# Attention and two MoE layers on one core: other planner constants, masks loaded first through another buffer, last output tile in halves

## The chip, the cores and the metric

The kernel runs on one core of a Trainium2 chip. The metric is the device time of one execution in microseconds (us). Three executions of the kernel before took 864.69, 868.79 and 866.26 us; their median is 866.26 us. One more was profiled and took 865.21 us, of which 863.4 us lie between its first and its last instruction (the span).

## The reference, cut to what matters

Inputs are q, k, v of shape (4 batches, 8 heads, 576 positions, 64), in float32, and weights in float64.

```
out_d     = softmax(mean4(q) @ mean4(k).T / 8) @ mean4(v)     # 144 pooled positions, repeated 4 times
out_local = softmax(where(|i - j| < 4, q @ k.T / 8, -1e9)) @ v  # a narrow band
x = (repeat4(out_d) + out_local), laid out as 2304 tokens x 512
h = x @ w_in (512 x 2048);   x = (h * cos(h)) @ w_out (2048 x 512)
out = ((x @ w1) * (x @ w2)) @ w3 @ w_out2    # 512 x 1024 twice, 1024 x 1024, 1024 x 512
```

## The kernel before, in words

**The work.** Weights arrive as 64-bit words and are turned into float32 on the chip: ScalarE and VectorE (`w_job`) take the two halves of each word apart and put a float32 together, three instructions for a block of 128 x 512. The products of the MoE layers run as three matmuls of split values (`mm3`). The last two weight matrices are first multiplied with each other (`w5_job`, tile `ps_w`, 128 matmuls of 128x512 in two halves r = 0 and 1), and the eight results go to a DRAM scratch `w5_sc` (shown as `w_sc`), issued by ScalarE. Attention is done by units of 192 positions (`unit_job`: the band) and by pairs of heads (`pair_job`: the pooled part, with `pool_v_job` for its values). Two units make a chunk of 384 tokens; a chunk's x feeds `h_job` (`ps_h`), a chain on ScalarE, VectorE and GpSimd (`chain_job`: turns, sine, square, g) and `y_job` (`ps_y`). After all six chunks the second layer runs (`ab_job`: `ps_ab`, `o_job`: `ps_o`), by three chunks of 768 tokens with six output tiles each.

**The planner.** Nothing is scheduled on the chip: while the program is built, a planner (`run`) keeps a clock for each engine, estimates every instruction (`cost`) and the delay until others see it (`LATENCY`), and gives each free engine the job with the lowest urgency whose inputs the plan holds ready. What comes out is a fixed order for each engine, and on the chip an engine that waits holds up all that stands behind it. The urgency of a job is a base plus one of the `U_` constants: of attention's loads of q and k, its pairs, its pooled values and its units, and of w_in, w_out and the second half of w3. The base of the first chunk's attention is `A0`; blocks j of the first half of w3 and of w4 have j - 0.5 and j - 1. Matmuls of `w5_job` have urgency 900, those of `h_job` 1016 and of `y_job` 1016.5, so on TensorE the product of the weights goes ahead of h where both are ready. `HALF` is the number of w_in blocks that chunk 0 goes through before chunk 1 starts. `SLACK` is how long a buffer must have been free in the plan before a load into it is issued. `exps` collects exponentials while ScalarE's table holds the sine, until `TOGETHER` of them wait or the first has waited `PATIENCE` ns. While TensorE has nothing to do early on, the planner puts matmuls of zeros there (`warm_up`, `ps_z`).

**The start.** ScalarE's queue issues six small DMAs: two for an identity matrix, four for the masks (`bands_raw`). SyncE issues q, k, v and weights, all on its own queue. `bands_raw` lies in buffer 0 of the ring `raw`; the same memory is taken next for `qkd`, the pooled q and k, which VectorE writes first of all. Then ScalarE casts the masks (`bands`) and scales the identity (`ident_r`); the first two units (`BANDS`) add the masks on TensorE and need both. 

**The end.** `o_out_job` copies a finished output tile from PSUM, on ScalarE for even tiles and VectorE for odd ones, and SyncE stores it.

Nearly every instruction is issued through the recorder at L131, so the profile's groups are told apart by tiles and not by lines; DMAs of ScalarE stand under L125.

Of the kernel before, what the change touches and what calls it, by code (L numbers as in the profile page):

```python
# [13 lines left out]
I64 = mybir.dt.int64  # L14
AF = mybir.ActivationFunctionType
# [6 lines left out]
P = 128  # L22
DM = H * D
# [12 lines left out]
QS = 64  # L36
KS = QS + 2 * HALO
# [5 lines left out]
N2 = 768  # L43
NH = N2 // 2
NCH2 = NT // N2
NQ = 7
HALF = 10
SCALE = 1.0 / math.sqrt(D)
TWO_PI = 2.0 * math.pi
LAG = 3  # L50
WARM = 256
EARLY_WARM, RISEN, REST = 3000.0, 10000.0, 130.0
FIRST, SLACK = 3000.0, 1000.0
TOGETHER, PATIENCE = 3, 6000.0
A0, A1 = 11, 4

U_QK, U_PAIR, U_POOL, U_UNIT = -13, -12, -11.5, -8
U_WI, U_WO, U_W3 = -4, -0.5, -1
OUT_BANKS = (4, 5, 6, 7, 2, 3)
EARLY = 2  # L60
BIAS, BANDS = 2, 4
LATENCY = {"pe": 200, "se": 140, "ve": 130, "ge": 150, "sy": 2000}


def band_of(u, w):
# [5 lines left out]
def fused_kernel(ctx: ExitStack, tc: tile.TileContext, qk_block, v_block, qk_pool, v_pool,  # L71
# [8 lines left out]
    def size(a):  # L80
        return math.prod(a.shape[1:])

    def cost(name, op, out, ins, func):
        n = max(size(a) for a in [out] + ins)
        if name == "ve":
            shared = n > 64 and ends["ge"] > max(now[0], ends["ve"])
            if op.startswith("tensor_scalar") and len(ins) == 1:
                return 90 + n * (1.5 if shared else 0.65)
            both = len(ins) == 2 and n > 64 and not any(a.tensor.name.startswith("ps_") for a in ins)
            return 75 + n * (2.2 if both and shared else 1.17 if both else 1.04)  # L90
        if name == "se":
            load = 1283 if func in (AF.Exp, AF.Sin) and func != table[0] else 0
            table[0] = func if load else table[0]
            return (60 if ins[0].tensor.name.startswith("ps_") else 100) + n / 1.2 + load
        if name == "ge":
            return 160 + (1.7 if any(0 in [step for step, _ in a.ap] for a in ins) else 2.3) * n
        if name == "sy":
            return max(450, n * out.shape[0] * (8 if out.dtype == I64 else 4) / 310)
        n = size(out)
        if op == "transpose":  # L100
            return 70
        if ins[0].dtype == F32R:
            return 12.5 + n / 2.4
        return (4 if ins[0].shape[0] == P else 2) * max(35, n / 2.4)

    def visible(a):

        end, by = written.get(a.tensor.name, (0.0, "pe"))
        return end + LATENCY[by]

# [24 lines left out]
    ve, se, pe, ge, sy = (Engine(*e) for e in (("ve", nc.vector), ("se", nc.scalar), ("pe", nc.tensor), ("ge", nc.gpsimd), ("sy", nc.sync)))  # L135
# [18 lines left out]
    ident_r = const.tile([P, P], F32R, name="ident_r")  # L154
    bands = const.tile([P, 3, KS], F32R, name="bands")
# [11 lines left out]
    def buf(slot, name, shape, dtype=F32):  # L167

        pool, size, _ = slots[slot[0]]
        item = 8 if dtype == I64 else 4  # L170
        t = pool.tile([P, size // item], dtype, name=name, tag=f"{slot[0]}{slot[1]}", bufs=1)
        t = t[:, :math.prod(shape)]
        if len(shape) == 1:
            return t
        names = "abcd"[:len(shape)]
        return t.rearrange(f"p ({' '.join(names)}) -> p {' '.join(names)}", **dict(zip(names, shape)))
# [27 lines left out]
    def on(name, fn, *aps, when=lambda: True):  # L204
        yield name, fn, aps, when

    def until(cond):
        while not cond():
            yield "until", cond
# [26 lines left out]
    def give(name, slot, engine):  # L236
        free[name].append((ends[engine] + LATENCY[engine], slot))

# [4 lines left out]
    def count(key, n=1):  # L243
        done[key] = done.get(key, 0) + n

    def reached(key, n):
        return lambda: done.get(key, 0) >= n
# [535 lines left out]
    def plan():  # L783

        f = 0
        while f < F1:
            if f >= HALF:
                yield from until(lambda: reached(("x", 1), UPC)() or ("wi", f) in w_t)
# [250 lines left out]

    def o_out_job(j, t, ps):  # L1040
        slot, name = (yield from take("t")), "ve" if t % 2 else "se"
        o = buf(slot, "o", [DM])
        yield from on(name, lambda: ve.tensor_copy(o, ps) if t % 2 else se.copy(o, ps), ps)
        give(f"bank{OUT_BANKS[t]}", 0, name)
        yield from on("sy", lambda: sy.dma_start(out=out[j * N2 + t * P:j * N2 + (t + 1) * P, :], in_=o), o)
        give("t", slot, "sy")
        count("out")

    with tc.manual_schedule():
        z = buf(("turns", 0), "zeros", [WARM])  # L1050
        ge.memset(z, 0.0)
        zr = z.bitcast(F32R)
        warmed = [(bank(7, "ps_z"), True)]

        def warm_up():

            if warmed[0] is None:
                if done.get("w5", 0) < F2 or not at_hand("bank7"):
                    return False
                ps, alone = bank(7, "ps_z"), True  # L1060
            else:
                ps, alone = warmed[0]
            pe.matmul(ps[:, :WARM], lhsT=zr[:, :P], rhs=zr, start=alone, stop=alone)
            ends["pe"] += REST if now[0] > RISEN else 0
            return True

        idle.append(warm_up)

        W5 = 2 * F2
        first, seen = {}, []  # L1070
        first.update({i: HALF if i == 1 else F1 * i for i in range(NC1)})
        first.update({("f", f): f if f < HALF else f + HALF for f in range(F1)})

        def attention(i, at):

            for b in sorted({(UPC * i + m) // UPB for m in range(UPC)} - set(seen)):
                seen.append(b)
                if b < EARLY:
                    for m in range(UPB):
                        Job(at + U_QK + 0.5 * m, unit_qk_job(UPB * b + m))  # L1080
                for p in range(KC):
                    Job(at + U_PAIR + 2 * p, pair_job(b, p))
                    Job(at + U_POOL + 2 * p, pool_v_job(b, p))
            for m in range(UPC):
                Job(at + U_UNIT + 3 * m, unit_job(UPC * i + m))

        ge.memset(ident, 0.0)
        se.dma_start(out=ident[:QB, :QB], in_=ident_in)
        se.dma_start(out=ident[QB:, QB:], in_=ident_in[:P - QB, :P - QB])
        raw = buf(("raw", 0), "bands_raw", [3, KS])  # L1090
        for half in (slice(0, QS), slice(QS, P)):
            se.dma_start(out=raw[half, :2], in_=bands_in[:QS, :2, :KS])
            se.dma_start(out=raw[half, 2], in_=bands_in[QB - QS:, 2, QB - QS:])
        se.copy(bands, raw)
        se.activation(out=ident_r, in_=ident, func=AF.Copy, scale=1.0 / SCALE)
        ends["sy"] = FIRST
        attention(0, A0)
        for j in range(F2):
            Job(j - 1, w_job(("w4", j), w4[j]))
            Job(j - 0.5, w_job(("w3", 0, j), w3t[0, j]))  # L1100
        for j in range(F2):
            Job(F2 + j + U_W3, w_job(("w3", 1, j), w3t[1, j]))
        Job(900, w5_job())
        for f in range(F1):
            Job(W5 + first["f", f] + U_WI, w_job(("wi", f), w_in[f]))
            Job(W5 + first["f", f] + U_WO, w_job(("wo", f), w_out[f]))
        Job(W5 + 1000, h_job(W5))
        Job(W5 + 1000.5, y_job())
        attention(1, W5 + first[1] - A1)
        for i in range(2, NC1):  # L1110
            run(reached("h", first[i - 1] + 1 if i > 2 else first[0] + HALF + 1))
            attention(i, W5 + first[i])
            if i == 2:
                for f in range(F2):
                    Job(W5 + first[2] + 4 * f, w12_job(f))
        run(lambda: done.get("h", 0) > first[NC1 - 1] and done.get("w12 begun", 0) == F2)
        at_stack.close()
        p2 = ctx.enter_context(tc.tile_pool(name="p2", bufs=1))
        slots.update({"x2": (p2, 4 * KC * N1, 6), "v": (p2, 4 * NH, 2)})
        free["x"] += [(0.0, ("x2", n)) for n in range(6)]  # L1120
        free["v"] = [(0.0, ("v", n)) for n in range(2)]
        base = W5 + NSTEPS
        for n in range(F2 * NQ // 2):
            Job(base + 2 * n / NQ - 8, back_job(n))
        for n in range(len(steps2)):
            Job(base + n - 6, w5_back_job(n))
        Job(base - 8, y_in_job(0))
        Job(base + 1000, ab_job(base))
        Job(base + 1000.5, o_job(base))
        run(reached("out", NT // P))  # L1130
# [53 lines left out]
```

## Time and profile before

| | us |
|---|---|
| median of 3 runs (lowest to highest) | 866.26 (864.69 to 868.79) |
| the profiled execution | 865.21 |
| its span | 863.4 |
| TensorE (PE) busy | 842.7 |
| VectorE (DVE) busy | 503.3 |
| ScalarE (ACT) busy | 446.9 |
| GpSimd (POOL) busy | 366.6 |

PE counts as busy while a matmul is in flight, and matmuls overlap; so the busy share says where PE had nothing at all, and the pace of a known group (a row "x12" with its length) says where it was slow. "Idle before" is followed by what ended it. In a timeline a row merges equal instructions that follow each other.

### The profile page before, as it was taken

Reading aid. Unit: us, or ns where it says so; the run is one execution under the profiler, and the core shown is the slowest. Engines: PE = TensorE matmul, PEld = TensorE weight load, DVE = VectorE, ACT = ScalarE, POOL = GpSimd, SP = SyncE. Lnnn points to the kernel's source line nnn. Section 1 sums busy time; section 2 is a strip of 40 time slices with the busy share of each in tenths; the row PEclk is TensorE's granted clock in tenths of the full one; section 3 lists DMA queues with packets and bytes.
Section 4 is the critical chain, followed back from the end, with each engine's and each line's share of the span. In section 5 each row is a group of like instructions: output and inputs, shape, how many; then the busy total and the mean of one; then the engine's idle time right before and its main releaser. Section 6 shows DMA issues by size and latency. Waiting matters only on the chain.

```text
span 863.4 us, 14938 instructions
## 1 busy us (share of the span) xinstructions
PE 842.7 (98%) x5627; PEld 760.4 (88%) x5627; DVE 503.3 (58%) x897; ACT 446.9 (52%) x908; POOL 366.6 (42%) x330
## 2 busy tenths in 40 slices
PE   8999989999999999999999999999999999999998
PEld 6454579989999899999999999999999899989997
DVE  5988687985537883787356434715335633364332
ACT  2655689876766775677667556651113311231111
POOL 0013677746442445245425344524334633363333
PEclk8999989999999999999999999999999999999999
DMA  9989982131446523555161329782000500021001
GB/s 277 294 252 349 311 251 81 59 114 49 143 145 202 172 87 110 177 163 158 56 212 52 110 101 352 278 296 72 24 25 25 171 25 25 13 71 52 25 25 73
DMA packets 59479, 118.24 MB, mean 137 GB/s; under 512 B 18232, under 2 KB 25400, under 8 KB 59408
## 3 DMA queue, kind: packets, MB, share of 16 engines
q1 hardware_dynamic: 53040, 108.76, 39.4%
q10 hardware_dynamic: 6368, 8.54, 2.8%
q8 instruction: 44, 0.72, 0.4%
q14 instruction: 27, 0.22, 0.1%
HBM read 89.49 MB, written 27.79 MB: 136 GB/s over the span
## 4 chain that ended last, share of the span: by engine, by line
PE 86%; DVE 5%; DMA 4%; ACT 2%; issue 1%; SPq 1%; POOL 0%; ACTq 0%; DVEq 0%; POOLq 0%
PE ps_h L131 21%; PE ps_y L131 21%; PE ps_ab L131 20%; PE ps_o L131 12%; PE ps_w L131 5%; DVE t L131 2%; PE ps_av L131 2%; PE ps_tb L131 2%; DMA w_sc<-w 1%; DMA raw<-w3t 1%; PE ps_p L131 1%; DMA kb<-qk_block 1%; PE ps_s L131 1%; PE ps_sb L131 1%; PE ps_t L131 1%
## 5 line engine op out<-in xcount | busy, mean ns | idle before, releaser
L131 PE MATMUL ps_h<-xs,wi 128*128 128x384 f32 x1152 | 225.3, 340 | 2.1 <-ACT up L131 1.8
L131 PE MATMUL ps_y<-g,wo 128*128 128x384 f32 x1152 | 222.5, 337 | 1.6 <-ACT yt L131 1.6
L131 PEld LDWEIGHTS ps_h<-xs,wi 128*128 128x128 f32 x1152 | 200.8, 189 | 6.6 <-issue 2.8
L131 PEld LDWEIGHTS ps_y<-g,wo 128*128 128x128 f32 x1152 | 199.6, 188 | 4.3 <-ACT yt L131 2.3
L131 PE MATMUL ps_ab<-y,w 128*128 128x384 f32 x1008 | 186.2, 337 | 1.7 <-ACT v L131 1.5
L131 PEld LDWEIGHTS ps_ab<-y,w 128*128 128x128 f32 x1008 | 176.7, 188 | 8.5 <-ACT v L131 2.1
L131 DVE TENSOR_TENSOR v<-v,ps_ab 128x384 f32<-128x384 f32 x168 | 90.7, 552 | 142.2 <-ACT w L131 73.5
L131 POOL TENSOR_TENSOR g<-c,g 128x384 fp32r<-128x384 f32 x96 | 104.2, 1086 | 158.2 <-ACT g L131 131.2
L131 ACT ACTIVATE c<-c 128x384 f32<-128x384 f32 x192 | 100.6, 524 | 35.0 <-DVE c L131 32.3
L131 POOL TENSOR_TENSOR v<-v 128x384 f32<-128x384 f32 x48 | 50.3, 1047 | 146.3 <-DVE v L131 145.5
L131 PE MATMUL ps_o<-w,m 128*128 128x512 f32 x432 | 107.8, 392 | 0.0
L131 ACT CAST m<-v 128x384 fp32r<-128x384 f32 x48 | 24.7, 515 | 157.0 <-POOL v L131 157.0
L131 DVE SCALAR_TENSOR_TENSOR c<-turns,ps_h 128x384 f32<-128x384 int32 x96 | 52.8, 550 | 72.6 <-ACT turns L131 65.3
L131 PEld LDWEIGHTS ps_o<-w,m 128*128 128x128 f32 x432 | 80.3, 188 | 13.8
L131 DVE SCALAR_TENSOR_TENSOR c<-c,ps_h 128x384 f32<-128x384 f32 x96 | 52.7, 549 | 56.3 <-ACT c L131 55.9
L131 ACT CAST g<-c 128x384 fp32r<-128x384 f32 x96 | 49.1, 512 | 44.1 <-DVE c L131 40.0
L131 ACT ACTIVATE turns<-ps_h 128x384 int32<-128x384 f32 x96 | 46.8, 488 | 40.5 <-PE ps_h L131 39.5
L131 PE MATMUL ps_w<-w,w 128*128 128x512 f32 x128 | 59.4, 604 | 0.4 <-DVE w L131 0.4
L131 ACT ACTIVATE t<-raw 128x512 f32<-128x512 f32 x72 | 47.3, 670 | 22.3 <-DMA raw<-w3t 8.5
L131 DVE TENSOR_SCALAR t<-t 128x512 int32<-128x512 int32 x72 | 46.5, 661 | 14.8 <-ACT t L131 14.6
L131 POOL TENSOR_TENSOR sc<-sc,bsum 128x840 f32<-128x840 f32 x12 | 22.6, 1884 | 64.8 <-DVE bsum L131 44.4
L131 POOL TENSOR_TENSOR m<-v,m 128x384 fp32r<-128x384 f32 x48 | 48.3, 1025 | 2.5 <-ACT m L131 2.5
(86 smaller groups left out, 871.5 us busy)
## 6 DMA issues: line engine op xcount, KB each, us to landing
w_sc<-w SPq DMA_DIRECT2D x56, 256.0 KB
w<-w_sc SPq DMA_DIRECT2D x28, 512.0 KB
raw<-w SPq DMA_DIRECT2D x24, 512.0 KB
raw<-w3t SPq DMA_DIRECT2D x16, 512.0 KB
raw<-w_in SPq DMA_DIRECT2D x16, 512.0 KB
raw<-w_out SPq DMA_DIRECT2D x16, 512.0 KB
w5r<-w_sc SPq DMA_DIRECT2D x24, 256.0 KB
kb<-qk_block SPq DMA_DIRECT2D x12, 408.0 KB
```

What stands on the lines that cost most here:

```text
L131: return call(*args, **kw)
```

## The change

The constants of the planner are set anew; the masks come into the buffer `st`, which is free at that time, the two DMAs of the masks that the first units use are the first in ScalarE's queue, and the cast is split in two; an exponential of one column of zeros stands ahead of the casts and brings ScalarE's exponential table; the last output tile is copied in halves by VectorE and ScalarE, and each half is stored by a queue of its own.

```diff
--- before
+++ after
@@ -44,22 +44,22 @@
 NH = N2 // 2
 NCH2 = NT // N2
 NQ = 7
-HALF = 10
+HALF = 11
 SCALE = 1.0 / math.sqrt(D)
 TWO_PI = 2.0 * math.pi
 LAG = 3
 WARM = 256
 EARLY_WARM, RISEN, REST = 3000.0, 10000.0, 130.0
-FIRST, SLACK = 3000.0, 1000.0
-TOGETHER, PATIENCE = 3, 6000.0
-A0, A1 = 11, 4
-
-U_QK, U_PAIR, U_POOL, U_UNIT = -13, -12, -11.5, -8
-U_WI, U_WO, U_W3 = -4, -0.5, -1
+FIRST, SLACK = 3000.0, 850.0
+TOGETHER, PATIENCE = 4, 6750.0
+A0, A1 = 6.0, 6
+
+U_QK, U_PAIR, U_POOL, U_UNIT = -13, -13, -10.5, -8.5
+U_WI, U_WO, U_W3 = -6, -1.0, -2.5
 OUT_BANKS = (4, 5, 6, 7, 2, 3)
 EARLY = 2
 BIAS, BANDS = 2, 4
-LATENCY = {"pe": 200, "se": 140, "ve": 130, "ge": 150, "sy": 2000}
+LATENCY = {"pe": 200, "se": 140, "ve": 130, "ge": 150, "sy": 2450}
 
 
 def band_of(u, w):
@@ -95,7 +95,7 @@
         if name == "ge":
             return 160 + (1.7 if any(0 in [step for step, _ in a.ap] for a in ins) else 2.3) * n
         if name == "sy":
-            return max(450, n * out.shape[0] * (8 if out.dtype == I64 else 4) / 310)
+            return max(450, n * out.shape[0] * (8 if out.dtype == I64 else 4) / 290)
         n = size(out)
         if op == "transpose":
             return 70
@@ -1039,10 +1039,18 @@
 
     def o_out_job(j, t, ps):
         slot, name = (yield from take("t")), "ve" if t % 2 else "se"
-        o = buf(slot, "o", [DM])
+        o, to = buf(slot, "o", [DM]), out[j * N2 + t * P:j * N2 + (t + 1) * P, :]
+        if (j, t) == (NCH2 - 1, N2 // P - 1):
+
+            halves = slice(0, DM // 2), slice(DM // 2, DM)
+            yield from on("ve", lambda: ve.tensor_copy(o[:, halves[0]], ps[:, halves[0]]), ps)
+            yield from on("se", lambda: (se.copy(o[:, halves[1]], ps[:, halves[1]]), se.dma_start(out=to[:, halves[1]], in_=o[:, halves[1]])), ps)
+            yield from on("sy", lambda: sy.dma_start(out=to[:, halves[0]], in_=o[:, halves[0]]), o)
+            count("out")
+            return
         yield from on(name, lambda: ve.tensor_copy(o, ps) if t % 2 else se.copy(o, ps), ps)
         give(f"bank{OUT_BANKS[t]}", 0, name)
-        yield from on("sy", lambda: sy.dma_start(out=out[j * N2 + t * P:j * N2 + (t + 1) * P, :], in_=o), o)
+        yield from on("sy", lambda: sy.dma_start(out=to, in_=o), o)
         give("t", slot, "sy")
         count("out")
 
@@ -1085,14 +1093,18 @@
                 Job(at + U_UNIT + 3 * m, unit_job(UPC * i + m))
 
         ge.memset(ident, 0.0)
+        raw = buf(("st", 0), "bands_raw", [3, KS])
+        for half in (slice(0, QS), slice(QS, P)):
+            se.dma_start(out=raw[half, :2], in_=bands_in[:QS, :2, :KS])
         se.dma_start(out=ident[:QB, :QB], in_=ident_in)
         se.dma_start(out=ident[QB:, QB:], in_=ident_in[:P - QB, :P - QB])
-        raw = buf(("raw", 0), "bands_raw", [3, KS])
         for half in (slice(0, QS), slice(QS, P)):
-            se.dma_start(out=raw[half, :2], in_=bands_in[:QS, :2, :KS])
             se.dma_start(out=raw[half, 2], in_=bands_in[QB - QS:, 2, QB - QS:])
-        se.copy(bands, raw)
+
+        se.activation(out=ident_r[:, :1], in_=z[:, :1], func=AF.Exp)
+        se.copy(bands[:, :2], raw[:, :2])
         se.activation(out=ident_r, in_=ident, func=AF.Copy, scale=1.0 / SCALE)
+        se.copy(bands[:, 2], raw[:, 2])
         ends["sy"] = FIRST
         attention(0, A0)
         for j in range(F2):
```

## Rows read from the trace of the kernel before

**Rows 1.** The page's busy times: engine, us, share of the span, instructions.
```profile
PE 842.7 (98%) x5627; PEld 760.4 (88%) x5627; DVE 503.3 (58%) x897; ACT 446.9 (52%) x908; POOL 366.6 (42%) x330
```

**Rows 2.** Windows: stretch, length, engines' busy us, granted clock, DMA share, GB/s.
```profile
0.00:20.00 20.00, 16.42 (x166) 14.59 (x167) 9.93 (x20) 3.64 (x6) 0.65 (x6) 0.83 0.92 266
20.00:40.00 20.00, 18.61 (x92) 9.86 (x91) 18.20 (x41) 12.94 (x37) 1.84 (x1) 1.00 1.02 310
...
80.00:100.00 20.00, 20.00 (x109) 9.72 (x108) 18.11 (x32) 12.22 (x28) 14.97 (x7) 1.00 1.01 329
100.00:120.00 20.00, 15.27 (x110) 12.95 (x109) 12.07 (x23) 14.93 (x35) 9.69 (x8) 0.83 0.99 303
```

**Rows 3.** Timeline of the start: start us, length, engine, operation [idle before].
```profile
2.16 2.72 ACTq L125 DMA_DIRECT2D bands_raw<-bands_in  x4
...
7.55 1.28 ACT L131 ACT_TABLE_LOAD   x1 [7.55 <-DMA bands_raw<-bands_in]
...
9.24 0.95 DVE L131 TENSOR_REDUCE qkd<-qb 128x192 f32<-128x768 f32 x1 [9.24 <-ACT bands L131]
...
9.47 0.70 PE L131 MATMUL ps_sb<-bands,ident_r 128*128 128x140 f32 x2 [2.49 <-ACT ident_r L131]
...
19.79 0.67 ACT L131 ACTIVATE t<-raw 128x512 f32<-128x512 f32 x1 [1.25 <-DMA raw<-w3t]
...
22.59 3.70 PE L131 MATMUL ps_w<-w,w 128*128 128x512 f32 x8
```

**Rows 4.** The chain of waits from 0 to 130 us: start, length, what.
```profile
2.16 4.36 DMA bands_raw<-bands_in
...
9.07 10.69 DMA raw<-w3t
...
32.05 0.64 PE ps_p L131 x8
...
34.55 0.50 PE ps_t L131 x8
...
98.21 6.53 DMA w_sc<-w
...
115.65 5.28 PE ps_h L131 x21
...
126.28 2.08 PE ps_h L131 x12
```

**Rows 5.** Timeline between the weights' product and the first h steps.
```profile
104.76 0.66 ACT L131 ACTIVATE t<-raw 128x512 f32<-128x512 f32 x1 [1.54 <-DMA w_sc<-w]
...
106.29 0.49 ACT L131 ACTIVATE turns<-ps_h 128x384 int32<-128x384 f32 x1
...
109.86 1.28 ACT L131 ACT_TABLE_LOAD   x1
...
112.68 1.07 PE L131 MATMUL ps_tb<-ident,sc 128*70 128x128 f32 x4 [2.16 <-ACT pt L131]
```

**Rows 6.** Windows of 2 us in the same stretch.
```profile
116.00:118.00 2.00, 2.00 (x8) 2.00 (x8) 1.38 (x3) 1.18 (x3) 2.00 (x2) 0.50 1.08 307
```

**Rows 7.** Timeline: a conversion alone, and one beside GpSimd's product.
```profile
26.41 0.42 DVE L131 TENSOR_SCALAR t<-t 128x512 int32<-128x512 int32 x1
...
27.39 1.84 POOL L131 TENSOR_TENSOR sc<-sc,bsum 128x840 f32<-128x840 f32 x1 [26.21 <-DVE bsum L131]
...
27.70 1.81 DVE L131 TENSOR_SCALAR t<-t 128x512 int32<-128x512 int32 x1
```

**Rows 8.** PE's waits from 115 to 580 us: total, times, longest.
```profile
PE ps_t L131 <- DVE sc L131: 2.1, 2, 1.5
```

**Rows 9.** Timeline of the end: the six stores and the last copy.
```profile
856.92 3.90 SPq L131 DMA_DIRECT2D out<-o  x6
...
859.78 0.69 DVE L131 COPY o<-ps_o 128x512 f32<-128x512 f32 x1 [0.74 <-PE ps_o L131]
```

**Rows 10.** A window at the end, after PE's last matmul.
```profile
859.90:860.90 1.00, 0.00 (x0) 0.00 (x0) 0.57 (x1) 0.00 (x0) 0.00 (x0) 1.00 1.00 387
```

## The prediction

> **What bounds the kernel now.** I read the page's busy times first. PE holds 842.7 of 863.4 us [rows 1], no other engine 60%, and the number of matmuls that compute something is the same after the change. So only the time in which PE has nothing, or runs slowly, can move: a change of order is worth at most what such places hold.
>
> The windows of 20 us come next, to find these places. Two of the first six stand out: 0 to 20 us, where PE's 16.42 us are to a good part matmuls of zeros, and 100 to 120 us, where PE is busy 15.27 us and the granted clock averages 0.83 [rows 2]. Between them PE is full (20.00 of 20 at 80 to 100 us), though with long matmuls. VectorE is the second engine there: 18.20 of 20 us at 20 to 40 us, 18.11 at 80 to 100 us; and the DMA engines' share is 1.0 [rows 2]. So early on PE, VectorE and the transfers are all near full, and what is put ahead pushes back something else.
>
> The timeline of the start shows why it is slow. VectorE's first instruction, the pooling of q, starts at 9.24 us, and not q ended its wait but the cast of the masks (the shared buffer). TensorE's first real matmul starts at 9.47 us, after 2.49 us of idle time, on `ident_r`. The cast itself waited for the masks' last DMA until 7.55 us and then for a table load of 1.28 us [rows 3]. The chain of waits has a second entry: the first block of w3t, issued at 9.07 us, takes 10.69 us to land [rows 4], its conversion on ScalarE starts at 19.79 us and the first product of weights at 22.59 us [rows 3].
>
> The same two views show the hole at 100 to 120 us. The product of the weights is over, its results go out with a store that takes 6.53 us [rows 4], and ScalarE waits 1.54 us for a buffer of that store with a conversion. The first `turns` of the h chain stands behind that and starts at 106.29 us, the sine's table is loaded at 109.86 us, and PE waits 2.16 us for a copy of ScalarE before the `ps_tb` at 112.68 us [rows 5]. The clock then falls to its lower level, 1.2 GHz (0.50 [rows 6]): 21 `ps_h` take 5.28 us where 12 take 2.08 us at 2.4 GHz, so 21 should take 3.64 us [rows 4].
>
> **The change part by part.**
>
> *Masks and exponential.* The masks leave the buffer that `qkd` needs, so VectorE waits for q alone. No row has q's landing; the nearest is the masks' first DMA, 4.36 us from an issue at 2.16 us [rows 4]. The q of unit 0 is the first load of SyncE's queue, so I take it as landed by 6.52 us: VectorE starts 2.7 us earlier. ScalarE issues the same six small DMAs. The table load of 1.28 us moves from behind the masks to beside their flight; this and the earlier masks let `ps_sb` start some 2 us earlier, into time that PE fills with zeros anyway, so by itself it is worth nothing. What counts is the first product of weights. It can't come before w3t lands at about 19.8 us: the first load of pooled values (urgency 11 - 11.5 = -0.5 before, 6 - 10.5 = -4.5 after) now goes ahead of w4's first block (-1) instead of ahead of w3's (-0.5), so w3's has the same bytes in front. From 19.79 to 22.59 us are 2.80 us; the conversion needs 0.67 us on ScalarE [rows 3] and two instructions of VectorE, at 0.42 us [rows 7] and, for lack of its row, 0.95 us (the pooling [rows 3]), together 2.04. The rest, 0.76 us, is queueing behind attention, which the earlier VectorE has done by then. Also the first pair's `ps_t` and `ps_p` (0.50 and 0.64 us [rows 4]) come into PE's empty time ahead of the first product, 1.14 us. Together 1.9 us off. Ends: nothing, if the landing sets everything; 2.7 us, if VectorE's whole shift passes through.
>
> *Attention of chunk 0 earlier (`A0`, `U_`).* Its pairs go from urgency -1 + 2p to -7 + 2p, its units from 3 and 6 to -2.5 and 0.5, ahead of nearly all weight blocks of the first half (j - 1, j - 0.5). w_in goes from 12 + f to 10 + f, w3's second half from 7 + j to 5.5 + j, w_out from 15.5 + f to 15 + f. In that stretch PE's sum of work doesn't change, and it is full from the first product to 100 us; so I count nothing there. What is changed is how much attention ScalarE and PE still have when the weights' product ends.
>
> *The hole at 100 to 120 us.* It holds 20 - 15.27 = 4.73 us of idle time [rows 2] and 5.28 - 3.64 = 1.64 us of half clock [rows 4], 6.4 us. h still stands behind the product of weights (1016 against 900), so the first h steps are still started when that is over, and their chain still needs a sine's table. But less of attention stands between, and the planner now takes a store to be visible 0.45 us later (2450 for 2000). I count the wait on the store (1.54 us) and PE's wait of 2.16 us [rows 5] as gone, 3.7 us, and leave the rest. What is late next is the h chain itself. Ends: nothing, or all 6.4 us; below nothing is a rival.
>
> *`HALF`, `A1`, `SLACK`, `TOGETHER`, `PATIENCE`, DMA rate.* One more step of chunk 0 before chunk 1 changes no count of matmuls. Four exponentials together instead of three save table loads of 1.28 us [rows 5] on ScalarE, which is busy 52% [rows 1]: hidden by PE. Later holes are few, as PE's 2.1 us for VectorE in pooled attention [rows 8]; some go, others come: 0, with 2.1 us either way.
>
> *The last tile.* Its copy of 0.69 us [rows 9] shrinks to about half, 0.35 us. But the six stores of 262,144 bytes are 1.57 MB, 4.06 us at the 387 GB/s of the last full window, where the DMA engines' share is 1.00 though no matmul runs [rows 10]. They are issued from 856.92 us over 3.90 us [rows 9], as fast as the engines take them; the sixth stands in line behind the fifth, and an earlier issue buys no earlier end. I take 0; ends 0.35 us off and, one more DMA at the mean pace of six in 3.90 us, 0.65 us on.
>
> [...]
>
> Sum: 1.9 + 3.7 = 5.6 us off. The profiled execution, 863.4 us of span in 865.21 us, would come to 859.6 us. It stands 1.05 us below the median of the runs; 866.26 - 5.6 = **860.7 us**.
>
> **The rivals.**
>
> A. *The hole only moves.* The h steps still start cold behind the product of weights, stores still hold buffers for 6.53 us against a plan of under 4, and ScalarE's order is as unlucky as before. For it: none of the urgencies at that point changes sign. Against: attention 0 is out of the way. Only 1.9 us are left: 864.4 us.
>
> B. *VectorE starves the product of weights.* Attention's instructions now go ahead of nearly all conversions, and VectorE has only 1.80 us free in 20 to 40 us [rows 2]. As soon as what it does ahead exceeds that, PE lacks a group of eight products, 3.70 us [rows 3], and the half clock adds 1.64 us as it did once [rows 4]; the start's gain is eaten and the hole stays: 866.26 + 5.3 = 871.6 us. Against it: attention brings its own matmuls, and VectorE starts 2.7 us earlier.
>
> What speaks for B in the rows: a conversion of 0.42 us takes 1.81 us beside GpSimd's product of 1.84 us [rows 7], and the units' two products now come amid more conversions. The skill ("SBUF — State Buffer", SBUF: two separate sides) calls the port pair of VectorE and GpSimd an exclusive lock that one holds for its whole instruction; the trace agrees, with 1.4 us lost at this place.
>
> C. *More is recovered.* The whole hole (6.4 us), the whole shift of VectorE (2.7 us) and a later wait (2.1 us [rows 8]): 11.2 us off, 855.1 us.
>
> **How the numbers follow.** Forecast 0.44, A 0.26, B 0.14, C 0.16. About 0.5% (4.3 us: below 861.9 or above 870.6) is what a measurement of this kernel can tell from no change. The forecast's own spread puts a fifth of it above 861.9 us; so faster is 0.35 + 0.16 + 0.02 of A = 0.53, the same 0.09 + 0.23 + 0.01 = 0.33, slower 0.14. The range reaches to C below and most of the way to B above: 854 to 869 us.
>
> **What would show it.** VectorE's first instruction before 7 us, on q and not on the masks; the first `ps_w` at 21 to 22 us; the window around the first h steps with PE over 18 of 20 us; the last DMA as late after the last matmul as now. I am wrong if PE idles over 2 us at 20 to 60 us (B), or if the first `turns` again comes over 5 us after the first `ps_h` (A).

## The result and the profile after

The changed kernel takes 856.48 us (median of 4 runs, 853.83 to 858.45) against 867.05 us before in the same comparison (4 runs, 864.69 to 868.79). The ratio is 0.9878, with a 95% interval of 0.984 to 0.9916: 10.6 us off, where 5.6 were forecast. The profiled execution is the slowest of the four, 858.45 us with a span of 856.7 us; the profiled one of before was below its median. So the two traces differ by 6.7 us only; what the rest is can be said only in part (the last section).

The page of the changed kernel, the row that answers to [rows 1]:

```profile
PE 839.6 (98%) x5645; PEld 758.4 (89%) x5645; DVE 502.9 (59%) x897; ACT 446.6 (52%) x911; POOL 366.2 (43%) x330
```

The windows of the changed kernel, with the columns of [rows 2]:

```profile
0.00:20.00 20.00, 15.93 (x172) 14.01 (x174) 12.18 (x24) 5.71 (x16) 0.91 (x7) 0.91 0.91 262
20.00:40.00 20.00, 18.45 (x114) 10.85 (x113) 19.40 (x45) 14.34 (x45) 3.18 (x2) 1.00 1.02 302
40.00:60.00 20.00, 19.70 (x152) 10.64 (x151) 15.23 (x30) 8.44 (x17) 1.46 (x1) 1.00 0.83 229
...
100.00:120.00 20.00, 17.58 (x110) 11.88 (x108) 12.50 (x23) 14.05 (x33) 10.24 (x8) 1.00 0.98 301
...
160.00:180.00 20.00, 19.66 (x155) 19.19 (x154) 20.00 (x30) 15.09 (x30) 15.34 (x11) 1.00 0.51 177
```

The hole at 100 to 120 us is smaller: 2.42 us of PE's idle time instead of 4.73, and the granted clock averages 1.00 instead of 0.83 [rows 2]. VectorE is fuller at 20 to 40 us (19.40 us for 18.20). And 160 to 180 us has become dense, a place that the prediction didn't look at. The kernel before has this there, first its window, then two rows of PE's timeline:

```profile
160.00:180.00 20.00, 18.05 (x141) 16.62 (x140) 20.00 (x26) 15.02 (x31) 16.03 (x12) 1.00 0.27 94
```
```profile
173.95 0.79 PE L131 MATMUL ps_y<-g,wo 128*128 128x384 f32 x3 [1.13 <-ACT yt L131]
175.22 1.31 PE L131 MATMUL ps_y<-g,wo 128*128 128x384 f32 x6 [0.48 <-ACT yt L131]
```

The start of the changed kernel, which answers to [rows 3]:

```profile
4.59 1.28 ACT L131 ACT_TABLE_LOAD   x1 [4.59 <-DMA bands_raw<-bands_in]
4.61 0.95 DVE L131 TENSOR_REDUCE qkd<-qb 128x192 f32<-128x768 f32 x1 [4.61 <-DMA qb<-qk_block]
...
7.23 0.45 PE L131 MATMUL ps_sb<-bands,ident_r 128*128 128x140 f32 x2
...
19.74 1.84 POOL L131 TENSOR_TENSOR sc<-sc,bsum 128x840 f32<-128x840 f32 x1 [18.56 <-ACT sd L131]
...
20.06 1.55 DVE L131 TENSOR_SCALAR sums<-sums 72x4 f32<-72x4 f32 x1
...
24.18 1.99 PE L131 MATMUL ps_w<-w,w 128*128 128x512 f32 x4 [1.55 <-DVE w L131]
```

VectorE begins at 4.61 us, on q, and the first matmul with the masks comes 2.2 us earlier. Yet the first product of weights comes at 24.18 us, 1.6 us later than before, and it waits for VectorE (1.55 us). Most of that lies at 20 us: VectorE's step of attention on `sums` (72x4) takes 1.55 us beside GpSimd's product of 1.84 us, where the same step took 0.17 us before, at 21.93 us with no such product beside it. It stands in VectorE's order ahead of the conversion that the first product needs.

The stretch after the product of weights, the rows that answer to [rows 5], of ScalarE and of PE, and one row of PE's before:

```profile
113.74 0.59 ACT L131 COPY w<-ps_w 128x512 f32<-128x512 f32 x1 [2.31 <-DMA w_sc<-w]
114.22 0.50 ACT L131 ACTIVATE turns<-ps_h 128x384 int32<-128x384 f32 x1
...
116.39 1.28 ACT L131 ACT_TABLE_LOAD   x1
```
```profile
108.71 1.08 PE L131 MATMUL ps_h<-xs,wi 128*128 128x384 f32 x3
109.64 0.66 PE L131 MATMUL ps_t<-ident,sd 72*72 72x72 f32 x8
110.10 3.91 PE L131 MATMUL ps_h<-xs,wi 128*128 128x384 f32 x21
115.78 0.71 PE L131 MATMUL ps_p<-ptp,vd 72*64 72x144 f32 x8 [1.77 <-DVE vd L131]
116.42 2.37 PE L131 MATMUL ps_h<-xs,wi 128*128 128x384 f32 x12
```
```profile
106.45 2.36 PE L131 MATMUL ps_h<-xs,wi 128*128 128x384 f32 x12 [1.82 <-ACT up L131]
```

ScalarE still waits for a store of the product, 2.31 us instead of 1.54, and the first `turns` still starts 5.5 us after the first `ps_h` (6.8 us before). But PE has something to do meanwhile: 24 `ps_h` and the rest of attention. Its waits for ScalarE of 1.82 us (the row before) and 2.16 us [rows 5] are gone; a wait of 1.77 us for VectorE is new. The row of 21 `ps_h` takes 3.91 us, at 2.4 GHz, where it took 5.35 us in the timeline before (5.28 us in the chain [rows 4]).

A table of when the same work starts makes the comparison by stage easy. "h+y #96" is the start of the 97th matmul of `ps_h` and `ps_y`, counted together in the timeline. The kernels from the third column on are experiments, told below: the constants alone, the order constants alone, and order with store constants.

| start, us | before | changed | all constants | order | order + store |
|---|---|---|---|---|---|
| first `ps_w` | 22.59 | 24.18 | 25.03 | 23.58 | 24.95 |
| last `ps_w` | 99.49 | 108.69 | 109.16 | 109.15 | 109.08 |
| x of chunk 1 complete | 150.57 | 128.28 | 126.95 | 126.95 | 127.14 |
| h+y #96 | 132.36 | 132.42 | 131.09 | 134.76 | 131.28 |
| h+y #192 | 153.84 | 150.11 | 148.78 | 152.07 | 149.00 |
| h+y #384 | 192.47 | 186.28 | 184.91 | 194.08 | 184.52 |
| h+y #1152 | 352.99 | 345.78 | 343.13 | 352.16 | 344.33 |
| h+y #1536 | 437.89 | 431.84 | 429.19 | 438.33 | 445.38 |
| first `ps_ab` | 580.52 | 575.04 | 571.40 | 580.54 | 591.93 |
| last `ps_o` | 859.28 | 852.05 | 848.67 | 859.01 | 868.82 |

Chunks are counted from 0. Read down the changed kernel's column against the first: level at #96, 3.7 us ahead at #192, 6.2 us at #384; nothing more until the second layer, which adds 1.8 us. At #96 it is level although x of chunk 1 is 22 us further: it has done attention that the kernel before still has ahead of it. So the 3.7 us at #192 were won before #96 and only show there: from #96 to #192 the kernel before has no idle time of PE and takes 21.48 us instead of 17.69, because it still does attention (`ps_t`, `ps_p`, `ps_tb`, `ps_av`) between its `ps_h` and `ps_y`. What is won after #96 itself are the 2.5 us from #192 to #384, mostly PE's waits for ScalarE's `yt` at 174 and 175 us (shown above), and what the second layer adds.

The end, which answers to [rows 9] and [rows 10], timeline and a window:

```profile
849.69 3.64 SPq L131 DMA_DIRECT2D out<-o  x6
...
852.54 0.42 DVE L131 COPY o<-ps_o 128x256 f32<-128x256 f32 x1 [0.74 <-PE ps_o L131]
853.00 0.37 ACT L131 COPY o<-ps_o 128x256 f32<-128x256 f32 x1 [0.62 <-DVE o L131]
853.41 0.34 ACTq L125 DMA_DIRECT2D out<-o  x1
```
```profile
853.70:854.70 1.00, 0.00 (x0) 0.00 (x0) 0.00 (x0) 0.00 (x0) 0.00 (x0) 1.00 0.95 353
```

The two halves are not copied side by side: ScalarE's waits for VectorE's, so both take 0.83 us where the whole copy took 0.69, and in the microsecond after that the DMA engines are still full (0.95).

### The profile page after: what moved, and what is told of

Same layout as the page of the kernel before. It is cut to its first block, busy times and chain, and to the rows that moved or that the text cites. A ratio compares the mean times of both kernels' runs of the same rounds, so it can differ in the third digit from the quotient of the medians.

```text
span 856.7 us, 14977 instructions
## 1 busy us (share of the span) xinstructions
PE 839.6 (98%) x5645; PEld 758.4 (89%) x5645; DVE 502.9 (59%) x897; ACT 446.6 (52%) x911; POOL 366.2 (43%) x330
## 4 chain that ended last, share of the span: by engine, by line
PE 83%; DVE 6%; DMA 5%; ACT 2%; issue 1%; ACTq 0%; POOL 0%; SPq 0%; DVEq 0%
PE ps_y L131 20%; PE ps_ab L131 20%; PE ps_h L131 19%; PE ps_o L131 12%; PE ps_w L131 5%; DVE t L131 2%; PE ps_av L131 2%; PE ps_tb L131 2%; DMA raw<-w3t 2%; DVE c L131 1%; PE ps_s L131 1%; DMA w_sc<-w 1%; PE ps_p L131 1%; DMA raw<-w_in 1%; PE ps_sb L131 1%
## 5 line engine op out<-in xcount | busy, mean ns | idle before, releaser
L131 PE MATMUL ps_h<-xs,wi 128*128 128x384 f32 x1152 | 219.5, 337 | 0.7 <-ACT ptp L131 0.5
L131 POOL TENSOR_TENSOR g<-c,g 128x384 fp32r<-128x384 f32 x96 | 106.5, 1109 | 157.1 <-ACT g L131 137.7
L131 PE MATMUL ps_w<-w,w 128*128 128x512 f32 x128 | 61.6, 608 | 1.5 <-DVE w L131 1.5
L131 DVE TENSOR_SCALAR t<-t 128x512 int32<-128x512 int32 x72 | 46.7, 662 | 11.2 <-ACT t L131 11.2
L131 POOL TENSOR_TENSOR xs<-xb,xs 128x512 fp32r<-128x512 f32 (+1 forms) x24 | 27.1, 1129 | 51.0 <-ACT xs L131 47.3
```

Source lines behind the costliest of these rows:

```text
L131: return call(*args, **kw)
```

## The experiments

Theory 1 was that the planner's constants carry the gain; theory 2 that the start's edit does or is needed; of the last tile I expected nothing. Four kernels were compared with the one before on one chip.

**The start's edit alone.**

```diff
-        raw = buf(("raw", 0), "bands_raw", [3, KS])
+        raw = buf(("st", 0), "bands_raw", [3, KS])
...
+        se.activation(out=ident_r[:, :1], in_=z[:, :1], func=AF.Exp)
```

> The kernel before with the start's edit alone (masks through the other buffer and first in their queue, split cast, exponential ahead); all constants as before. Theory 1 (the gain is the planner's constants; the start edit only lets VectorE begin at about 4.6 us): the first product of weights hangs on the landing of w3t, so 0 to 1 us off, ratio 0.999 to 1.000. Theory 2 (the start edit passes VectorE's whole shift of 4.6 us on to the product): first ps_w 3 to 4 us earlier, ratio about 0.996.

Measured: 865.05 us, ratio 0.9985 (0.9961 to 1.0008). Timeline of this kernel, VectorE's first instruction and PE's first product with what stands ahead of it:

```profile
4.53 0.95 DVE L131 TENSOR_REDUCE qkd<-qb 128x192 f32<-128x768 f32 x1 [4.53 <-DMA qb<-qk_block]
```
```profile
20.04 1.95 PE L131 MATMUL ps_s<-qkd 64*72 64x144 f32 x8 [1.17 <-ACT sd L131]
21.91 4.63 PE L131 MATMUL ps_w<-w,w 128*128 128x512 f32 x5
```

VectorE starts 4.7 us earlier, the first product 0.68 us (22.59 before). What the product hangs on is the landing of w3t, at 18.6 us instead of 19.8 (ScalarE waits 0.87 us for it); of these 1.2 us half a microsecond is lost again, as the 8 `ps_s` that stand ahead in PE's order take 1.95 us at 1.2 GHz (granted clock 0.50 at 18 to 24 us in this trace). Alone, the edit can't be told from nothing.

**The last tile in halves alone.**

```diff
+        if (j, t) == (NCH2 - 1, N2 // P - 1):
+            yield from on("ve", lambda: ve.tensor_copy(o[:, halves[0]], ps[:, halves[0]]), ps)
...
```

> The kernel before with the last tile in halves alone. Theory 1 (the stores' queue is full at the end, and the halves have shorter rows): no gain, up to 0.6 us slower, as the trace after shows 3.45 us from the last matmul's start to the last packet against 2.90 before. Theory 2 (the shorter copy counts): 0.3 us faster. Both inside 0.1%; it is read from the end of the trace.

Measured: 865.03 us, ratio 1.0 (0.9985 to 1.0016). From the last `ps_o`'s start to the end of the span it takes 4.12 us, before 4.07. Here too ScalarE's half waits for VectorE's:

```profile
863.22 0.37 ACT L131 COPY o<-ps_o 128x256 f32<-128x256 f32 x1 [0.62 <-DVE o L131]
```

**All constants alone, and the change without the halves.**

> The kernel before with the planner's constants alone. Theory 1: the whole gain or nearly so, ratio 0.988 to 0.991, x of chunk 1 ready some 20 us earlier. Theory 2 (start and constants need each other: VectorE must begin early for attention to go ahead): less than half of it, ratio 0.994 or more, first ps_w later than 25 us.

> The changed kernel with the last tile copied and stored whole again. Theory 1: equal to the changed kernel or up to 0.5 us faster, ratio 0.987 to 0.988. Theory 2: 0.3 us slower than the changed one.

Measured: 855.37 us, ratio 0.9881 (0.9862 to 0.9901), and 854.41 us, ratio 0.9864 (0.9843 to 0.9886). Theory 1 holds: the constants alone give the change's ratio, and neither the start nor the halves add anything that these intervals show. Of theory 2 one sign came, the first product later than 25 us, without costing the gain. The constants alone put the first product at 25.03 us, with the start's edit 24.18: here the start's edit is worth 0.85 us at that point.

**Which constants?** Four kernels with a part of them each.

```diff
# order
+HALF = 11
+A0, A1 = 6.0, 6
+U_QK, U_PAIR, U_POOL, U_UNIT = -13, -13, -10.5, -8.5
+U_WI, U_WO, U_W3 = -6, -1.0, -2.5
# store
+FIRST, SLACK = 3000.0, 850.0
+LATENCY = {"pe": 200, "se": 140, "ve": 130, "ge": 150, "sy": 2450}
+            return max(450, n * out.shape[0] * (8 if out.dtype == I64 else 4) / 290)
# exponentials
+TOGETHER, PATIENCE = 4, 6750.0
# A0 alone
+A0, A1 = 6.0, 4
```

> The kernel before with A0, A1, HALF and the U_ urgencies of the change, and nothing else. Theory 1 (the gain comes from attention of the first two chunks lying ahead of and under the product of weights): x of chunk 1 ready at about 127 us as with all constants, ratio 0.988 to 0.992. Theory 2 (it comes from the plan's longer delay of a store, so that ScalarE no longer stands behind stores): x of chunk 1 early as well, but the hole after the product of weights stays near 7 us and the ratio is 0.995 or more.

> The kernel before with LATENCY of a transfer 2450, 290 GB/s and SLACK 850 alone. Theory 1: within 0.3% of before. Theory 2: at least half of the gain, ratio 0.994 or less, and the wait of ScalarE on the store of the weights' product (1.54 us before) gone.

> The kernel before with TOGETHER 4 and PATIENCE 6750 alone. Theory 1: within 0.3% of before; the first 115 us as before, the pauses at 240 to 300 us may move by 2 us either way. Theory 3 (exponentials in larger groups take PE's waits at 240 to 300 us away): 3 us off, ratio 0.996.

> The kernel before with A0 6 for 11 alone: attention of chunk 0 ahead, all else as before. Theory 1 in its narrow form (attention 0 is what stood in the hole): first ps_w about 2 us later, x of chunk 0 some 8 us earlier, ratio 0.990 to 0.994. Rival (w_in and attention of chunk 1 have to come earlier too): x of chunk 1 not more than 8 us earlier than the 150.6 us of before, hole as before, ratio 0.997 to 1.002.

| | us | ratio | 95% |
|---|---|---|---|
| order | 865.5 | 1.0005 | 0.9977 to 1.0033 |
| store | 882.7 | 1.0178 | 1.0115 to 1.0242 |
| exponentials | 865.18 | 0.9982 | 0.9948 to 1.0016 |
| A0 alone | 871.43 | 1.0074 | 1.0049 to 1.0099 |
| all three groups | 855.37 | 0.9881 | 0.9862 to 0.9901 |

The exponentials alone do nothing, as expected. For order, theory 2's ratio (0.995 or more) came, but not its sign, a hole that stays near 7 us: PE's two waits there are 1.32 and 1.56 us. The ratios of store and of A0 alone came as no theory had them. No group alone makes the kernel faster, and the parts' ratios say nothing of the whole: theory 1 in the form that attention ahead carries the gain by itself is refuted. The table of starts shows what the order does: x of chunk 1 is as early as with all constants (126.95 us), but the lead is lost before #96 and at 154 to 194 us. So theory 4: the order of the first chunks and the plan's time of a transfer must change together.

**Order with store constants, and their halves.**

```diff
# order + store: both groups of above
# order + transfer's time: order, LATENCY 2450 and 290 GB/s, SLACK as before
# the change without it
-            return max(450, n * out.shape[0] * (8 if out.dtype == I64 else 4) / 290)
+            return max(450, n * out.shape[0] * (8 if out.dtype == I64 else 4) / 310)
-LATENCY = {"pe": 200, "se": 140, "ve": 130, "ge": 150, "sy": 2450}
+LATENCY = {"pe": 200, "se": 140, "ve": 130, "ge": 150, "sy": 2000}
# the change with the last tile whole and
+LATENCY = {"pe": 200, "se": 140, "ve": 130, "ge": 150, "sy": 2900}
```

> The kernel before with the order constants (A0, A1, HALF, U_) and the store constants (LATENCY of a transfer 2450, 290 GB/s, SLACK 850) together; exponentials as before. Theory 4 (each group alone gains nothing because the order of the first two chunks and the plan's time of a transfer must change together): the gain to within 0.3%, ratio 0.987 to 0.991, lost time of PE at 154 to 192 us near 1 us. Rival (the constants work only all together, by chance of the later chunks): ratio 0.994 or more, though the first 220 us are as in the changed kernel.

> Order constants with LATENCY 2450 and 290 GB/s, SLACK as before. Theory 4: what matters of the store constants is the transfer's time, so the same as with SLACK, ratio 0.987 to 0.992. Rival (SLACK carries it): ratio 0.996 or more.

> The changed kernel with LATENCY of a transfer 2000 and 310 GB/s as before, all else changed. Theory 4: most of the gain is lost, ratio 0.994 to 1.002, and PE loses 5 us or more at 154 to 192 us. Rival (the transfer's time in the plan does not matter once the order is set): ratio 0.987 to 0.990.

> The changed kernel with the last tile whole and LATENCY of a transfer 2900 for 2450. If the gain comes from the plan lying nearer to the landings on the chip (6 to 11 us in the first 120 us), a longer delay gains as much or more: ratio 0.983 to 0.988. If 2450 is only a value at which the later stages happen to fit, ratio 0.992 or more.

| | us | ratio | 95% |
|---|---|---|---|
| order + store | 874.46 | 1.0111 | 1.0082 to 1.014 |
| order + transfer's time | 863.28 | 0.9979 | 0.9963 to 0.9995 |
| change, transfer's time as before | 865.14 | 0.9996 | 0.9976 to 1.0016 |
| change, whole tile, 2900 | 869.43 | 1.0045 | 1.0023 to 1.0068 |

One of the four came as theory 4 had it: without the longer transfer the change's gain is gone, and what goes is lost where it was expected (from #192 to #384 42.98 us instead of 36.17). In that kernel PE's timeline at 160 to 178 us has the first three rows here, and the changed kernel the last one:

```profile
167.61 0.33 PE L131 MATMUL ps_sb<-kb,qb 64*64 64x70 f32 x2 [1.75 <-DVE c L131]
169.32 1.67 PE L131 MATMUL ps_sb<-kb,qb 64*64 64x70 f32 x46 [1.38 <-DVE sc L131]
170.92 4.14 PE L131 MATMUL ps_y<-g,wo 128*128 128x384 f32 x12
```
```profile
172.26 0.95 PE L131 MATMUL ps_sb<-kb,qb 64*64 64x70 f32 x46 [0.34 <-DVE sc L131]
```

A unit's scores stand in PE's order before VectorE has done the steps that they wait for; VectorE has no pause there up to 175 us, and in the changed kernel none at all (20.00 of 20 us). PE waits 1.75 and 1.38 us, the granted clock averages 0.83 at 160 to 180 us, and 12 `ps_y` take 4.14 us. The kernel with the order constants alone has the same two waits there. In the changed kernel the same scores are placed later and wait 0.34 us. The x of chunk 1 is as early (126.47 us) and #384 is 8.3 us later (194.58 against 186.28 us).

For order with store the rival came: it is slower than before, though its start is like the changed kernel's. Its column in the table says where: 8.7 us ahead at #1152, where the change is 7.2 us ahead, and 7.5 us behind at #1536, 11.4 us at the first `ps_ab`. PE's timeline of that kernel, and windows of it and of the kernel with all constants:

```profile
421.64 6.53 PE L131 MATMUL ps_y<-g,wo 128*128 128x384 f32 x36
435.24 2.77 PE L131 MATMUL ps_tb<-ident,sc 128*70 128x128 f32 x12 [7.07 <-POOL sc L131]
437.94 1.98 PE L131 MATMUL ps_av<-pt,vb 70*64 70x64 f32 x32
442.23 1.13 PE L131 MATMUL ps_av<-pt,vb 70*64 70x64 f32 x16 [2.31 <-ACT t L131]
445.38 7.10 PE L131 MATMUL ps_h<-xs,wi 128*128 128x384 f32 x24 [2.03 <-POOL xs L131]
```
```profile
425.00:445.00 20.00, 8.98 (x79) 7.58 (x77) 7.33 (x13) 9.30 (x16) 4.96 (x6) 0.64 0.56 181
445.00:465.00 20.00, 18.20 (x172) 17.33 (x173) 11.19 (x20) 10.75 (x21) 7.04 (x8) 0.84 0.43 134
```
```profile
425.00:445.00 20.00, 20.00 (x118) 20.00 (x117) 10.04 (x19) 13.52 (x29) 7.34 (x7) 1.00 0.54 165
445.00:465.00 20.00, 20.00 (x200) 19.35 (x199) 13.26 (x24) 12.73 (x22) 7.89 (x8) 1.00 0.58 184
```

PE has finished chunk 3's steps and chunk 4's attention is not there yet: 11.02 us without work, then 24 `ps_h` in 7.10 us, where a row of 24 takes 4.32 us with all constants, because the clock fell (0.64, 0.84). ScalarE's timeline of that kernel has the reason, an exponential that starts when PE is already empty. In ScalarE's order it stands behind four copies `yt`, the first of which waits 3.50 us for PE's last `ps_y`:

```profile
426.65 1.01 ACT L131 ACTIVATE yt<-ps_y 128x384 f32<-128x384 f32 x2 [3.50 <-PE ps_y L131]
...
428.27 0.49 ACT L131 ACTIVATE yt<-ps_y 128x384 f32<-128x384 f32 x1
...
429.72 1.28 ACT L131 ACT_TABLE_LOAD   x1
431.02 0.90 ACT L131 ACTIVATE sc<-sc 128x840 f32<-128x840 f32 x1
```

A hole stands at this place in other kernels too. PE is busy in 425 to 445 us as follows, with the store constants alone, with order and the transfer's time, and with 2900:

```profile
425.00:445.00 20.00, 12.33 (x116) 11.23 (x116) 9.24 (x18) 11.79 (x23) 7.48 (x7) 0.86 0.61 204
```
```profile
425.00:445.00 20.00, 14.84 (x118) 13.53 (x120) 4.12 (x9) 9.37 (x19) 7.42 (x8) 0.91 0.47 155
```
```profile
425.00:445.00 20.00, 13.67 (x133) 12.33 (x130) 6.80 (x11) 8.53 (x18) 8.76 (x8) 0.78 0.50 163
```

It is not the same hole. With the store constants alone PE waits 7.7 us for the same product of GpSimd; with order and the transfer's time 4.3 us for GpSimd's `xs`; with 2900 2.5 us for a load of values and 1.8 us for `xs`. A0 alone has one as well (14.96 of 20 us busy).

So theory 4 is right up to 345 us and wrong for the whole. SLACK doesn't carry the gain: with it, order is 11 us slower (874.46 against 863.28). The constants of the exponentials, worth nothing alone, are what takes this hole away when they join the other two groups; that is shown, since order + store and all constants differ in nothing else. Why the plan puts that exponential so late wasn't tried, nor which of `TOGETHER` and `PATIENCE` it is, nor the two other groups without the order: whether the order is needed stays open. And a transfer's time of 2900 opens a hole at this place again: the value of 2450 is not better because it lies nearer to the chip's landings, as the expectation had allowed.

The second layer's 1.8 us go with the transfer's time in the plan. From the first `ps_ab` to the last `ps_o` it takes 276.9 to 277.3 us in the traces of all kernels that have 2450 or 2900, and 278.5 to 279.7 us in those of all that have 2000.

The best kernel of the study is the change with the last tile stored whole (0.9864); from the change itself (0.9878) its interval doesn't set it apart.

## Why the prediction was right and where it was not

*The forecast.* 856.48 us lie in the range, the direction is right, and 10.6 us are nearly twice the 5.6 forecast; rival C's 11.2 is closer in size. That the time came out so near is in part luck: in the traces, the stages that the 5.6 us were counted for gave 3.7, and 3.5 more came from stages that stood at 0. Of the four signs, VectorE's early start on q came; the first `ps_w` at 21 to 22 us (24.18) and PE over 18 of 20 us around the first h steps (17.58) did not; and the trace ends 4.6 us after the last `ps_o`'s start instead of 4.1.

*Masks and exponential: 1.9 us off.* Alone, the step is right in its first half: VectorE began 4.7 us earlier (2.7 taken). The product came 0.68 us earlier (0.76 worked out), but that is luck: the queueing between landing and product, which was to shrink from 2.8 to 2.0 us, was 3.3 us, and it was the landing, taken as fixed, that came 1.2 us earlier. The 1.14 us of attention did not come into the empty start: in the changed kernel the first `ps_t` is at 26.00 us, behind the first product.

*"So I count nothing there", on attention going ahead.* This failed. With the constants alone the first product is 2.44 us later, because conversions stand behind attention on VectorE, rival B's mechanism at a small size; 1.4 us of it are lost beside GpSimd's product, as B had it (1.55 us for a step of 0.17). B itself didn't come: PE was idle 1.85 us at 20 to 60 us, just under its mark.

*The hole: 3.7 of 6.4 us.* 4.73 us idle and a fallen clock became 2.42 us idle and a full clock, 4.0 us back. The size was right, the reason only in part: PE's wait of 2.16 us went, but the wait on the store didn't, it grew to 2.31 us, and it was ScalarE's and not PE's. The chain's start came only 1.3 us nearer, and my mark for rival A (over 5 us from the first `ps_h` to the first `turns`) was met, at 5.5 us, without A being true. What changed is that chunk 1's attention was mostly done, under the product of weights.

*Later stages: 0.* This is the term that was mis-sized. From #192 to #384 the changed kernel gains 2.5 us, and the second layer gains 1.8 us; 0.7 us are lost between them. I had named one later wait of PE [rows 8] and let the rest cancel. A short wait can also cost more than its length, as the experiment without the longer transfer shows: 3.1 us of waits at 166 to 169 us, with the clock's fall behind them, go with 6.8 us from #192 to #384.

*Costing the constants one by one.* I gave each group a price of its own and summed. The runs refute that: +0.05%, +1.78% and -0.18% alone, -1.19% together.

*The last tile: 0.* Right, and the trace bears out the reason given: the DMA engines are full there. That the halves run one after the other I hadn't seen.

## What to carry to other kernels

In a kernel whose engines follow an order fixed by a plan, a constant of the plan has no price of its own: try the constants together, and look in the trace for the one place where the order and the chip disagree, since a single late instruction can take back 20 us. Look for what PE can do while a chain is slow to start, instead of making the chain faster. An edit that issues the last store earlier bought nothing here, where the transfers were already full; look at their share first.

## What the runs showed of the hardware

The granted clock may be a large part of the difference. Each run lists its mean; twice one minus it, times the run's time, is the time at 1.2 GHz. In the 27 runs of the kernel before of the last comparison that mean is 0.9908, or 15.9 us at 1.2 GHz, and over these runs a further us at 1.2 GHz goes with 0.49 us of time (correlation 0.82). The changed kernel's four runs have a mean of 0.9975, or 4.3 us. The difference of 11.6 us would be some 5.7 of the 10.6 us by that slope; the kernel before's 23 and 25 runs beside the earlier experiments give slopes of 0.32 and 0.60, so this is rough, 4 to 7 us. It is a correlation: no run changed the clock alone. Order constants alone had 0.9939, or 10.6 us, and were no faster. And not all of it costs: in the profiled run of the kernel before about half of the time at 1.2 GHz lies in the first 20 us [rows 2], where PE runs many matmuls of zeros.

In all traces the dips between the first products and the end come with or after pauses of PE, as at the 7.07 us above. But the same pause isn't always followed by one. At 280 to 300 us the kernel before and the two with one edit alone (start, last tile) all have the same 2.1 us of waits on `ps_t` and 17.91 us of work; the granted clock there is 1.00 before and 0.83 in the two others, and from #384 to #1152 they take 163.5 and 163.6 us instead of 160.5. So two executions of the same plan can differ by 3 us in this way.
